# A shorter lead for the unit loads of a fused attention and feed-forward kernel, from the preparation of unit 11 on

## The chip, the cores and the metric

One core of one Trainium2 chip. The metric is the device time of one execution in microseconds (us). Most executions of one kernel agree within 0.3%, so each kernel was timed in several rounds, next to the kernel before on the same chip. A **ratio** in this document is the mean time of one kernel's fast runs over that of the other's of the same rounds, so it is not quite the ratio of the medians that are quoted beside it. Runs that fell into a slower state of the chip are left out of ratios.

The engines: PE multiplies matrices, PEld is its weight load, ACT and DVE do element-wise work, POOL is a further element-wise engine, SP issues nearly all DMAs. "SPq" in the profile is SP's sequencer. A DMA *lands* when all its data has arrived; its window on SP ends earlier. The *lead* is how many units ahead of the prepared one the loads are issued.

## The reference

Decaying linear attention over blocks, then a bilinear feed-forward layer. Cut to what matters:

```python
# q, k, v: (4, 8, 768, 64); lam: (8,)
for b in range(nb):                       # blocks of the sequence
    intra = (q_b @ k_b.T * Dmask) @ v_b   # decay within the block
    inter = (q_b * lam_pow) @ kv_state    # everything earlier
    out_b = intra + inter
    kv_state = lam_block * kv_state + (k_b * rev_pow).T @ v_b
x = out.reshape(3072, 512)
result = ((x @ w_a) * (x @ w_b)) @ w_out  # 512 -> 1536 -> 512
```

## The kernel before

The sequence is cut into 24 units of 128 rows (4 batches of 6). The units are put together in groups; while PE runs the feed-forward layer of one group, the attention of later units is slipped in at fixed slots of the plan. Each unit needs three loads (q, k, v, 256 KB each), a scaling of k and q on POOL, a cast of v on DVE, and a transpose of the scaled pair. From unit 11 on that transpose is a DMA. The parts that the change touches:

```python
GROUPS = (4, 1, 2, 4, 4, 4, 4, 1)
LOOKAHEAD = 3
DMA_T_FROM = 11
...
# plan of group 3 (units 7 to 10): slot, piece, unit. P prepares, S and Q hold scores
# (1, "P", 13), (3, "S", 11), (3, "S", 12), (3, "P", 14),
# (7, "Q", (11, 12, 13, 14)), (10, "P", 15), (12, "P", 16), (16, "Q", (13, 14, 15, 16))
...
ld_pool = tile_pool(name="ld", bufs=4)          # four buffers each for q, k, v
...
    def load_x(w, u):
        ...
        nc.sync.dma_start(out=t, in_={"q": qr, "k": kr, "v": vr}[w][b, nb])   # L126
...
    def pump():                                  # issues what may be issued now
        while pending:
            kind, c = pending[0]
            if kind in "abo":
                ...                              # weights, all done early on
            elif c >= used["u"] + LOOKAHEAD:
                return
            pending.pop(0)
            ...
                load_x(kind, c)
...
    def prep_k(u):
        make_ks(u, ...)                          # POOL, L257
        make_qs(u, "pool")                       # POOL, L262
        used["u"] = u + 1
        if u >= DMA_T_FROM:
            ...
            nc.sync.dma_start_transpose(...)     # L280

    def prep_v(u):
        make_vb(u, ...)                          # L271
        pump()                                   # loads of u + 3 follow the transpose of u
```

So SP meets, for each prepared unit u, first the transpose of u, then the three loads of unit u + 3, all in one in-order stream with the stores of the results.

## Time and profile before

| | |
|---|---|
| time of the first three runs | 235.88, 236.29, 240.94 us |
| median with later rounds of the same session | 236.31 us (6 runs) |
| span of the profiled execution | 234.4 us |
| PE busy | 226.4 us, 97% |
| wait of PE for a transposed unit | one, near 101 us |

The lines that carry this stand in the prediction below. The list of waits of PEld between 70 and 200 us of the kernel before has this line (total, times, longest):

```profile
PEld L308 <- DMA qkT<-qk: 1.5, 1, 1.5
```

The next two lines are busy time by stretch, one for 95 to 105 us and one for 86 to 98 us, of the kernel before. Columns: stretch, its length, then busy time and instructions of PE, PEld, DVE, ACT and POOL; the last two numbers are the share of 16 DMA engines and GB/s:

```profile
95.00:105.00 10.00, 8.68 (x74) 4.46 (x72) 6.57 (x11) 3.34 (x7) 2.04 (x2) 1.00 1.34 184
...
86.00:98.00 12.00, 12.00 (x70) 5.55 (x69) 7.96 (x13) 3.67 (x7) 4.09 (x4) 1.00 1.24 247
```

PE lacks 1.3 us in the first stretch. From 86 to 98 us the DMA engines are booked beyond their number (1.24) and move 247 GB/s. The share is the time that packets took, counted where they start; a high share alone doesn't prove a high rate.

### The profile page before, as it was taken

The numbers are of one execution on the slowest core, as the hardware profiler recorded it, in microseconds if no ns is written. First come the engines' busy times: TensorE is split into PE (matmuls) and PEld (weight loads), VectorE is DVE, ScalarE is ACT, GpSimd is POOL, SyncE is SP. The second block draws the span as 40 slices with busy tenths as digits, with TensorE's granted clock in tenths as the row PEclk, the third lists the DMA queues.
The fourth block names the chain that finished last, engine by engine and source line by source line (L and its number), as shares of the span: only waits on it lengthen the run. The fifth ranks groups of instructions, "written<-read, shape, count | busy, mean of one in ns | idle before, by whom it ended". The sixth has DMA issues, their size and how long they took to land.

```text
span 234.4 us, 4575 instructions
## 1 busy us (share of the span) xinstructions
PE 226.4 (97%) x1791; PEld 125.6 (54%) x1791; DVE 114.5 (49%) x204; ACT 93.0 (40%) x174; POOL 49.6 (21%) x65
## 2 busy tenths in 40 slices
PE   7799999999999999979999999999999999999994
PEld 2474444459689554444544454544454544444493
DVE  0896557536459627664144574135574224332050
ACT  3585753066364443332243342243342233432261
POOL 6061000237245544130333330030300000000000
PEclk9999999999999999999999999999999999999999
DMA  4999999999998999999719969415050220000311
GB/s 153 302 286 350 347 366 282 294 214 292 215 235 183 228 200 254 188 203 231 174 45 222 181 105 229 121 68 111 0 48 0 89 88 6 0 0 6 131 48 46
DMA packets 94278, 38.32 MB, mean 163 GB/s; under 512 B 81200, under 2 KB 89776, under 8 KB 94256
## 3 DMA queue, kind: packets, MB, share of 16 engines
q1 hardware_dynamic: 94112, 38.02, 70.8%
q8 instruction: 14, 0.23, 0.5%
q14 instruction: 8, 0.07, 0.1%
q10 hardware_dynamic: 144, 0.00, 0.0%
HBM read 28.32 MB, written 6.29 MB: 148 GB/s over the span
## 4 chain that ended last, share of the span: by engine, by line
PE 88%; DMA 6%; ACT 2%; DVE 1%; SPq 1%; issue 1%; DVEq 0%
PE op L453 26%; PE a_ps L432 26%; PE b_ps L432 25%; DMA k<-in_k_dram 3%; PE o_ps L350 3%; DMA qkT<-qk 2%; PE kq L308 2%; PE o_ps L340 2%; PE kvd L364 2%; PE tps L294 1%; DVE m L325 1%; ACT o_sb L448 1%; SPq L207 1%; PE kq L565 1%; ACT xT L357 0%
## 5 line engine op out<-in xcount | busy, mean ns | idle before, releaser
L444 DVE TENSOR_TENSOR ab<-a_sb,b_ps 128x512 bf16<-128x512 bf16 (+2 forms) x96 | 52.5, 552 | 80.9 <-PE b_ps L432 58.5
L432 PE MATMUL a_ps<-xT,wa_sb 128*128 128x512 bf16 (+2 forms) x384 | 77.2, 326 | 0.6 <-ACT xT L357 0.6
L432 PE MATMUL b_ps<-xT,wb_sb 128*128 128x512 bf16 (+2 forms) x384 | 77.3, 326 | 0.0
L439 ACT CAST a_sb<-a_ps 128x512 bf16<-128x512 f32 (+2 forms) x96 | 45.6, 481 | 62.4 <-PE a_ps L432 61.5
L453 PE MATMUL op<-wo_sb,ab 128*128 128x512 bf16 (+2 forms) x312 | 65.6, 363 | 0.0
L432 PEld LDWEIGHTS <-wb_sb 128*128 128x128 bf16 x384 | 34.5, 98 | 28.6
L432 PEld LDWEIGHTS <-wa_sb 128*128 128x128 bf16 x384 | 33.8, 98 | 29.0 <-POOL wa_sb L160 0.6
L453 PEld LDWEIGHTS <-ab 128*128 128x128 bf16 x312 | 28.7, 98 | 29.9
L325 DVE TENSOR_TENSOR m<-kq,lotri 128x512 bf16<-128x512 f32 x47 | 29.4, 682 | 19.0 <-PE kq L308 18.7
L257 POOL TENSOR_TENSOR qk<-kf,lp_k 128x512 bf16<-128x512 f32 x18 | 18.9, 1051 | 79.3 <-PE kvd L364 30.9
L448 ACT COPY o_sb<-op 128x512 f32<-128x512 f32 (+2 forms) x26 | 14.2, 554 | 37.8 <-PE op L453 37.8
L262 POOL TENSOR_TENSOR qk<-qf,lp_q 128x512 bf16<-128x512 f32 x20 | 21.0, 1051 | 23.0 <-DMA qf<-in_q_dram 23.0
L357 ACT CAST xT<-o_ps 128x512 bf16<-128x512 f32 x22 | 12.0, 590 | 18.4 <-PE o_ps L350 17.9
L396 DVE TENSOR_TENSOR st<-kvd,bdiag 128x512 bf16<-128x512 f32 x18 | 12.3, 682 | 4.9 <-PE kvd L364 3.8
L296 ACT COPY qkT<-tps 128x1024 bf16<-128x1024 bf16 x7 | 7.1, 1012 | 10.7 <-PE tps L294 10.7
L195 PE MATMUL idle<-idle_sb 128*128 128x128 bf16 (+1 forms) x31 | 7.4, 380 | 1.3 <-DVE idle_sb L190 1.3
L308 PE MATMUL kq<-qkT 64*128 64x128 bf16 x160 | 6.7, 218 | 1.3 <-DMA qkT<-qk 1.3
L350 PE MATMUL o_ps<-m,vb 128*64 128x128 bf16 x192 | 7.9, 222 | 0.0
L271 POOL CAST vb<-vf 128x512 bf16<-128x512 f32 x7 | 4.6, 651 | 14.1 <-DMA vf<-in_v_dram 12.8
L271 DVE CAST vb<-vf 128x512 bf16<-128x512 f32 x17 | 7.5, 441 | 0.0
L340 PEld LDWEIGHTS <-st 128*128 128x128 bf16 x80 | 5.4, 98 | 2.8
L350 PEld LDWEIGHTS <-vb 128*64 128x64 bf16 x192 | 5.8, 109 | 1.4
(56 smaller groups left out, 85.8 us busy)
## 6 DMA issues: line engine op xcount, KB each, us to landing
vf<-in_v_dram SPq DMA_DIRECT2D x24, 256.0 KB, 4.9
out_dram<-o_sb SPq DMA_DIRECT2D x23, 256.0 KB, 2.0
qf<-in_q_dram SPq DMA_DIRECT2D x20, 256.0 KB, 4.2
kf<-in_k_dram SPq DMA_DIRECT2D x20, 256.0 KB, 4.7
wst<-in_moe_w_a_dram SPq DMA_DIRECT2D x6, 512.0 KB, 8.8
wst<-in_moe_w_b_dram SPq DMA_DIRECT2D x6, 512.0 KB, 8.8
wst<-in_moe_w_out_dram SPq DMA_DIRECT2D x6, 512.0 KB, 8.5
q<-in_q_dram SPq DMA_DIRECT2D x2, 512.0 KB, 5.5
```

What stands on the lines that cost most here:

```text
L257: eng_of(eng).tensor_mul(qk[:, 1], raw.pop((u, "k")), lp_k[:, u % NB].to_broadcast([128, H, D]))
L262: eng_of(eng).tensor_mul(U[u]["qk"][:, 0], raw.pop((u, "q")), lp_q[:, u % NB].to_broadcast([128, H, D]))
L271: eng_of(eng).tensor_copy(vb, vf)
L325: nc.vector.tensor_mul(m, kq[i], lotri_bc)
L350: nc.tensor.matmul(d["o"][p, hp, :], lhsT=d["vb"][:, 2 * hp + i, :], rhs=d["m"](i, hp), start=(first and hp == 0), stop=True, skip_group_c ...
L357: nc.scalar.copy(xT[:, :, col:col + BLK], o_ps)
L396: nc.vector.tensor_mul(st[:].rearrange("p hp i d -> p hp (i d)"), ps[:].rearrange("p hp i d -> p hp (i d)"), bdiag_bc)
L432: nc.tensor.matmul(ps[:, :gt], lhsT=w_sb[:, s, f * 128:(f + 1) * 128], rhs=xT[:, s, :gt], start=(s == 0), stop=(s == KS - 1))
L439: nc.scalar.copy(a_sb[:, :gt], ps[:, :gt])
L444: nc.vector.tensor_mul(ab[:, f, :gt], a_sb[:, :gt], ps[:, :gt])
L448: nc.scalar.copy(o_sb[:, lo:hi], op[:, lo:hi])
L453: nc.tensor.matmul(op[:, lo:hi], lhsT=ab[:, f, t * 128:(t + 1) * 128], rhs=wo_sb[:, f, lo:hi], start=(f == 0), stop=(f == FC - 1))
```

## The change

The intent is to issue the loads of the later units closer to their use: from the preparation of unit 11 on, a unit's loads are issued when the unit two before it has been prepared, not three. Everything else stays.

```diff
-LOOKAHEAD = 3
+LOOKAHEAD = (3, 2)
...
-            elif c >= used["u"] + LOOKAHEAD:
+            elif c >= used["u"] + LOOKAHEAD[used["u"] > DMA_T_FROM]:
```

## The prediction

> **What bounds the kernel now.** I read the page first, then who waits for whom, then the timeline around the one wait that matters, then the sequencer that issues the DMAs. The page's first part says that the matrix engine is the bound:
>
> ```profile
> PE 226.4 (97%) x1791; PEld 125.6 (54%) x1791; DVE 114.5 (49%) x204; ACT 93.0 (40%) x174; POOL 49.6 (21%) x65
> ```
>
> The span is 234.4 us, so PE idles 8.0 us in all. Busy time by stretch puts 3.0 of these after 200 us (34.00 less 31.03) and the rest before 60 us, apart from one place: between 60 and 200 us only the stretches 95 to 100 (4.70 of 5.00) and 100 to 105 (3.98 of 5.00) are not full. The list of waits of PE, limited to 70 to 200 us, holds a single line:
>
> ```profile
> PE kq L308 <- DMA qkT<-qk: 1.3, 1, 1.3
> ```
>
> So everything that an earlier or later load of units 12 to 23 can give in the body of the kernel is this 1.3 us, unless it makes a new wait. The timeline shows it in the middle of the score products of two units, eight for unit 13 and eight for unit 14:
>
> ```profile
> 99.30 0.40 PE L308 MATMUL kq<-qkT 64*128 64x128 bf16 x8
> 101.02 0.40 PE L308 MATMUL kq<-qkT 64*128 64x128 bf16 x8 [1.32 <-DMA qkT<-qk]
> ```
>
> The data needed is the transposed q and k of unit 14 (the plan of group 3 has the scores of 13 and 14 at slot 7). The chain that ended last goes back to where that transpose came from:
>
> ```profile
> 95.14 5.84 DMA qkT<-qk
> 100.97 0.05 issue
> 101.02 0.40 PE kq L308 x8
> ```
>
> So the transpose of unit 14 started at 95.14 and took 5.84 us to land. Columns in the next fence: start in us, time, engine and line. The timeline of SP alone shows why it started so late. Each line is one DMA, L126 a load of q, k or v, L280 a transpose, L449 a store. Counting transposes from the first (unit 11), these are 11, 12, 13 and 14, and the triples of loads are units 14, 15 and 16:
>
> ```profile
> 79.38 2.94 SPq L280 DMA_TRANSPOSE qkT<-qk  x1
> 82.38 0.56 SPq L126 DMA_DIRECT2D qf<-in_q_dram  x1
> 82.99 0.58 SPq L126 DMA_DIRECT2D kf<-in_k_dram  x1
> 83.67 1.02 SPq L126 DMA_DIRECT2D vf<-in_v_dram  x1
> 84.79 0.85 SPq L449 DMA_DIRECT2D out_dram<-o_sb  x1
> 85.74 1.35 SPq L280 DMA_TRANSPOSE qkT<-qk  x1
> 87.14 0.57 SPq L126 DMA_DIRECT2D qf<-in_q_dram  x1
> 87.77 0.89 SPq L126 DMA_DIRECT2D kf<-in_k_dram  x1
> 88.75 0.73 SPq L126 DMA_DIRECT2D vf<-in_v_dram  x1
> 89.58 1.14 SPq L449 DMA_DIRECT2D out_dram<-o_sb  x1
> 90.83 1.67 SPq L280 DMA_TRANSPOSE qkT<-qk  x1
> 92.55 0.60 SPq L126 DMA_DIRECT2D qf<-in_q_dram  x1
> 93.20 0.70 SPq L126 DMA_DIRECT2D kf<-in_k_dram  x1
> 94.01 1.02 SPq L126 DMA_DIRECT2D vf<-in_v_dram  x1
> 95.14 2.32 SPq L280 DMA_TRANSPOSE qkT<-qk  x1
> ```
>
> The gaps between lines are 0.05 to 0.1 us: from 79.38 on SP issues without rest, in program order, and each instruction occupies it for 0.6 to 3 us. Yet the transpose's input was there long before, as the timeline of POOL shows for unit 14:
>
> ```profile
> 87.28 1.04 POOL L257 TENSOR_TENSOR qk<-kf,lp_k 128x512 bf16<-128x512 f32 x1 [3.18 <-PE a_ps L432]
> 88.28 1.04 POOL L262 TENSOR_TENSOR qk<-qf,lp_q 128x512 bf16<-128x512 f32 x1
> ```
>
> It was ready at 89.32 and waited 5.8 us for its turn. In this stretch **SP's issue order is the local bound**, not the data.
>
> **What the Trainium skill says.** "Perfetto Trace Analysis", section "DMA Instruction — HWDGE (DVE, Sync)": the profiled window of such a DMA begins when its semaphores are satisfied and ends when the sequencer is free again; the movement of the data lies outside. The trace agrees: the transpose has 2.32 us on SP and lands 5.84 us after its start. The same page, "What "DMA-bound" means", names a sequencer track that is solid DMA slices as one of the ways to be bound by DMA; the lines above are that. "DMA: Bandwidth & Descriptors", "Issuing engines are not separate DMA queues", calls the issue time usually small beside the DMA itself; here a triple of loads holds SP for 2.4 to 2.6 us against a landing of 3.5 to 6.1 us, so it is not small.
>
> **The change part by part.** No compute instruction is added or removed; the order of ACT and POOL is identical, and the differences on PE and DVE are buffer numbers. All 60 q, k and v loads of the later units remain. On SP each load triple from unit 14 on is issued one preparation step later: the order transpose 11, load 14, store, transpose 12, load 15, store, transpose 13, load 16, transpose 14 becomes transpose 11, store, transpose 12, load 14, store, transpose 13, load 15, transpose 14. So **one triple less stands ahead of transposes 12, 13 and 14**: about 2.45 us each (84.79 less 82.38 is 2.41, 89.58 less 87.14 is 2.44, 95.14 less 92.55 is 2.59). What was moved falls later into slack.
>
> The new times, with the durations shown: store at 82.4 (its copy on ACT ended at 81.24), transpose 12 at 83.3 (its input ended at 80.52), load 14 at 84.7 to 87.1, store at 87.1, transpose 13 at 88.3 (input ended at 84.10), load 15 at 90.0 to 92.5, transpose 14 not before 92.5. Its input now comes later too: k of unit 14 issues at about 85.3 and lands after 4.1 to 4.7 us (the landing times of k loads in this stretch), so 90.0; POOL then needs 1.04 for k and 1.0 for q, done at 92.1. Both conditions give 92.5 where it was 95.14, some 2.6 us earlier. With the same 5.84 us it lands at 98.4. PE reaches unit 14's products at 99.70 (101.02 less 1.32). The 1.32 us wait goes, with 1.3 us to spare.
>
> Is there a new wait? I followed each later unit. Unit 15: loaded by 97, POOL done at 97.4, needed at 116.3. Unit 16: load after transpose 14, data at 100, and POOL starts k at 102.45 anyway because it waits for PE to free a buffer. Units 17 and 18: loads at 100 and about 108, POOL took them up at 112.17 and 117.75. Unit 19: the load at 124.0 lands at 128.6, POOL ends at 131, its transpose ran at 135.93 because it waited 5.0 us for PE. Unit 20: issued at 128.7, lands at 133.5, POOL ends at 136, transpose at 139.76. Units 21 and 22: 142 and 147 against a transpose at 157.46 and a POOL start at 152.62. Unit 23: load after transpose 21, 158.8 to 161.2, lands at 166; its transpose waits for PE until about 170 anyway. It pushes transpose 22 from 158.84 to about 161.2, landing at 166, needed at 170.79. All have 3 us or more. **Sum: 1.3 us off, 0 on**, so 236.3 becomes 235.0.
>
> **The rivals.** First, **the load becomes the wait**: with only two units of lead, unit 14's k load may land late, POOL is late and transpose 14 issues at 95 or after. For it: POOL waited for a k load four times in the whole run (6.6 us), one of them just before (1.49 us at 82.01), and the wait ahead of k of unit 14 ended at 87.28, just when the load of 82.99 with its 4.1 us landed. Against: there are 2.6 us of gain to eat up first. It would give 236 to 238. Second, **the DMA engines and not SP are the bound**: the DMA share of the stretches from 80 to 110 is above 1.2, and SP's windows of 2 to 3 us for a transpose look like back-pressure. Then transpose 12, directly behind transpose 11 and a store, would take up to 2.9 instead of 1.35 us, transpose 14 would start at about 94 and land at 99.7, and the gain would be near zero to 1.3: 235.0 to 236.2. In its favour for the change, less data stands ahead of transpose 14 in that case too, since 768 KB of loads are moved behind it. Third, a lucky case: beyond the wait, fewer collisions speed up nothing on PE, as its products run at a fixed pitch (0.86 us for four) and its clock is full; so no gain over 1.5 us is plausible.
>
> **Range and chances.** Median before is 236.29, of three runs of which one (240.94) stands apart; the two others average 236.1. I take 235.0. Low end 234.3: full gain from the lower of the two fast runs would be 234.6, less 0.3 for scatter. High end 236.4: no gain, or a partial gain and scatter. Within 2% means 231.6 to 241.0: a gain over 4.7 us has no idle time to come from, so faster gets 0.01; a loss over 4.7 us needs several new stalls or a slow run as median: 0.02.
>
> **What would show it.** Right: PE has no wait at line 308 between 70 and 200 us, busy time is full from 95 to 105, transpose 14 starts near 92.5 and lands before 99, and everything after 100 us is earlier by 1.3 us to the end, with a span near 233.1. Wrong: a wait for the transpose remains (then look whether POOL or SP held it), or a new wait of PE for a transpose appears near 116, 134, 151 or 170, or POOL waits for loads on the way to a late transpose.

## The result, and the profile after

| | before | after |
|---|---|---|
| median | 236.31 us (6 runs, 235.88 to 240.94) | 234.57 us (6 runs, 234.51 to 234.68) |
| span in the profile | 234.4 us | 232.9 us |
| ratio of fast runs, 95% interval | | 0.9927, 0.9913 to 0.9941 |

The gain is 0.7%: real, as the interval shows, and within the 2% that count as the same.

The list of waits of PE between 70 and 200 us no longer has a line for a transpose. The timeline of PE in the kernel after shows the scores of units 13 and 14 as one run of 16 products where there were two of eight:

```profile
99.02 0.39 PE L340 MATMUL o_ps<-qkT,st 128*128 128x128 bf16 x4
99.34 0.62 PE L308 MATMUL kq<-qkT 64*128 64x128 bf16 x16
99.89 0.64 PE L350 MATMUL o_ps<-m,vb 128*64 128x128 bf16 x16
```

In the kernel before, the first eight products began at 99.30 and those of L350 at 101.34; here they begin at 99.34 and 99.89. So 1.49 us vanish in this one place (2.04 from products to L350 before, 0.55 after). That is the whole difference of the spans, 1.5 us. Busy time by stretch, kernel after, the same two stretches:

```profile
95.00:105.00 10.00, 9.95 (x79) 5.12 (x79) 7.50 (x12) 3.90 (x7) 3.70 (x4) 1.00 1.36 207
...
86.00:98.00 12.00, 11.95 (x70) 5.51 (x69) 8.07 (x13) 3.71 (x7) 4.46 (x4) 1.00 1.27 246
```

PE is full (9.95 of 10.00). From 86 to 98 us the DMA engines are as full as before: the work has changed its order, not its amount. The two microseconds after that stretch differ; they are taken up after the experiment act_beside. The timeline of SP in the kernel after shows the new order (L280 transposes 11, 12, 13, 14; L126 the loads of units 14 and 15; L449 stores):

```profile
79.05 2.12 SPq L280 DMA_TRANSPOSE qkT<-qk  x1
81.30 0.48 SPq L449 DMA_DIRECT2D out_dram<-o_sb  x1
81.89 2.08 SPq L280 DMA_TRANSPOSE qkT<-qk  x1
84.02 0.57 SPq L126 DMA_DIRECT2D qf<-in_q_dram  x1
84.64 0.63 SPq L126 DMA_DIRECT2D kf<-in_k_dram  x1
85.37 0.90 SPq L126 DMA_DIRECT2D vf<-in_v_dram  x1
86.37 0.88 SPq L449 DMA_DIRECT2D out_dram<-o_sb  x1
87.35 1.33 SPq L280 DMA_TRANSPOSE qkT<-qk  x1
88.73 0.57 SPq L126 DMA_DIRECT2D qf<-in_q_dram  x1
89.35 1.01 SPq L126 DMA_DIRECT2D kf<-in_k_dram  x1
90.45 0.84 SPq L126 DMA_DIRECT2D vf<-in_v_dram  x1
91.41 2.12 SPq L280 DMA_TRANSPOSE qkT<-qk  x1
```

Transpose 14 starts at 91.41, 3.7 us earlier than before, and takes 4.5 us to land in place of 5.84. It lands at 95.9, and PE needs it at 99.6 (99.34 and half of the 0.55 us that the 16 products take). What the shorter lead costs is visible on POOL, which now waits longer for k loads, among them those of unit 14 (first line) and of unit 19 (third):

```profile
88.96 1.23 POOL L257 TENSOR_TENSOR qk<-kf,lp_k 128x512 bf16<-128x512 f32 x1 [5.09 <-DMA kf<-in_k_dram]
90.16 1.04 POOL L262 TENSOR_TENSOR qk<-qf,lp_q 128x512 bf16<-128x512 f32 x1
...
127.79 1.29 POOL L257 TENSOR_TENSOR qk<-kf,lp_k 128x512 bf16<-128x512 f32 x1 [9.46 <-DMA kf<-in_k_dram]
```

POOL is done with unit 14 at 91.20, 0.2 us before SP turns to its transpose, and with unit 19 at 130.08, while its transpose starts at 134.47. Nothing on PE waits for either.

### The profile page after: what moved, and what is told of

Read it like the earlier page. It is cut to its first block, busy times and chain, and to the rows that moved or that the text cites. A ratio compares the mean times of both kernels' runs of the same rounds, so it can differ in the third digit from the quotient of the medians.

```text
span 232.9 us, 4552 instructions
## 1 busy us (share of the span) xinstructions
PE 224.7 (96%) x1768; PEld 125.6 (54%) x1791; DVE 116.0 (50%) x204; ACT 92.9 (40%) x174; POOL 50.3 (22%) x65
## 4 chain that ended last, share of the span: by engine, by line
PE 92%; DMA 3%; ACT 2%; issue 1%; SPq 1%; DVE 0%
PE a_ps L432 27%; PE b_ps L432 27%; PE op L453 26%; DMA k<-in_k_dram 3%; PE o_ps L350 3%; PE kq L308 2%; PE o_ps L340 2%; PE kvd L364 2%; PE tps L294 1%; ACT o_sb L448 1%; SPq L207 1%; PE kq L565 1%; ACT xT L357 0%; PE kv L364 0%; PE tk L529 0%
## 5 line engine op out<-in xcount | busy, mean ns | idle before, releaser
L453 PE MATMUL op<-wo_sb,ab 128*128 128x512 bf16 (+2 forms) x300 | 64.1, 362 | 0.9 <-issue 0.5
L262 POOL TENSOR_TENSOR qk<-qf,lp_q 128x512 bf16<-128x512 f32 x20 | 21.5, 1076 | 23.4 <-DMA qf<-in_q_dram 23.4
L271 DVE CAST vb<-vf 128x512 bf16<-128x512 f32 x17 | 9.3, 549 | 0.0
L350 PE MATMUL o_ps<-m,vb 128*64 128x128 bf16 x192 | 7.9, 222 | 0.0
L340 PEld LDWEIGHTS <-st 128*128 128x128 bf16 x80 | 5.4, 98 | 2.8
L350 PEld LDWEIGHTS <-vb 128*64 128x64 bf16 x192 | 5.8, 109 | 1.4
```

Of the source, the lines that this page charges most:

```text
L262: eng_of(eng).tensor_mul(U[u]["qk"][:, 0], raw.pop((u, "q")), lp_q[:, u % NB].to_broadcast([128, H, D]))
L271: eng_of(eng).tensor_copy(vb, vf)
L350: nc.tensor.matmul(d["o"][p, hp, :], lhsT=d["vb"][:, 2 * hp + i, :], rhs=d["m"](i, hp), start=(first and hp == 0), stop=True, skip_group_c ...
L453: nc.tensor.matmul(op[:, lo:hi], lhsT=ab[:, f, t * 128:(t + 1) * 128], rhs=wo_sb[:, f, lo:hi], start=(f == 0), stop=(f == FC - 1))
```

## The experiments

The theories. **A**: SP works through its DMAs in order, and the time that it spends on issuing loads 14 to 16 is what delays transpose 14. **C**: the later loads (units 17 to 23) share in the gain. **D**: what helped is that loads 14 and 15 no longer crowd transposes 12 and 13. **E**: the DMA engines are the limit, and data of loads ahead of or beside the transpose delays it, whoever issues them.

Twelve runs on the chip, all with correct results. "T14" is transpose 14: its start on SP, its time to land, and the wait of PEld for a transpose in the profile.

| run | T14 start | to land | wait | median | before, same rounds | ratio |
|---|---|---|---|---|---|---|
| before (first profile) | 95.14 | 5.8 | 1.5 | 236.31 | | |
| after | 91.41 | 4.5 | none | 234.57 | 236.31 | 0.9927 |
| before_again | 95.38 | 6.1 | 2.0 | 236.33 | 236.23 | 0.9967 |
| head_only | 91.30 | 4.6 | none | 234.61 | 236.23 | 0.9904 |
| tail_only | 95.28 | 5.7 | 1.4 | 236.20 | 236.23 | 0.9963 |
| one_triple | 92.4 | 4.1 | none | 234.68 | 236.23 | 0.9909 |
| load14_late | 95.75 | 5.6 | 1.8 | 236.04 | 235.68 | 1.0021 |
| act_queue | 94.6 | 6.7 | 1.5 | 235.85 | 235.68 | 1.0007 |
| two_all | 94.11 | 6.4 | none | 235.16 | 235.68 | 0.9977 |
| one_ahead | 94.58 | 4.7 | 0.8 (T16) | 235.59 | 235.68 | 0.9998 |
| act_beside | 92.4 | 7.1 | none | 234.22 | 235.91 | 0.9934 |
| small_issues | 94.11 | 5.5 | none | 235.05 | 235.90 | 0.9966 |
| small_again | 93.97 | 6.3 | 0.8 | 235.03 | 235.91 | 0.9970 |
| pool_queue | after 98 | | 5.7 | 241.17 | 235.90 | 1.0196 |

The rounds of the first four (236.23) had three runs of before at 238.2 to 238.8 us that pull the ratios down: the unchanged kernel itself came out at 0.9967 there. For these four the medians are the better guide. The kernel before has a median of 235.68 to 236.31 us, depending on the rounds, so a run is best compared with its own rounds.

### before_again: the same kernel once more

No edit but a comment.

> The unchanged kernel, profiled once more. Theory A (issue order on SP delays transpose 14): transpose 14 starts at about 95 us again and PE waits for it around 101 us; the length of that wait varies from run to run, by up to 1 us either way of 1.5 us, which would explain why the timed gain (1.7 us) is larger than the wait in the one profile (1.5 us) and why the kernel before scatters more than the changed one. Rival: the wait is an accident of the one profile; then it is absent here and the gain comes from elsewhere. Time 236.3 us under both.

The wait is there again, and longer (waits of PEld between 70 and 200 us):

```profile
PEld L308 <- DMA qkT<-qk: 2.0, 1, 2.0
```

The span is 234.9 us where the first profile had 234.4: the 0.5 us of extra wait is the 0.5 us of extra span. So the wait is no accident, its length varies with the execution, and between these two executions that variation goes straight into the time. The kernel after has no such wait; its six runs lie within 0.17 us.

### head_only and tail_only: which part of the change does it

```diff
 head_only
-            elif c >= used["u"] + LOOKAHEAD:
+            elif c >= used["u"] + (2 if 12 <= used["u"] <= 14 else LOOKAHEAD):
 tail_only
-            elif c >= used["u"] + LOOKAHEAD:
+            elif c >= used["u"] + (2 if used["u"] >= 15 else LOOKAHEAD):
```

> Two units of lead at the preparations of units 11, 12 and 13 only, and again three from unit 15 on: the order on SP is that of the changed kernel up to transpose 14, and that of the kernel before from transpose 15 on. Theory A: the whole gain, 234.6 us, ratio 0.993, transpose 14 starts near 91.5 us and PE has no wait for it. Rival C (the later loads, units 17 to 23, share in the gain because the DMA engines are less loaded there): only a part, 235.0 to 236 us.

> The complement: three units of lead up to the preparation of unit 13, two from unit 14 on. The order on SP up to transpose 14 is that of the kernel before. Theory A: no gain, 236.3 us, ratio 1.000 within 0.002, transpose 14 near 95 us, the PE wait of about 1.5 us stays. Rival C: a part of the gain, 235 to 236 us.

The head alone gives 234.61 us, the tail alone 236.20 us, where the change as a whole gave 234.57 and the kernel before 236.23 in these rounds. The timeline of PE of the tail-only kernel still has the gap:

```profile
99.38 0.40 PE L308 MATMUL kq<-qkT 64*128 64x128 bf16 x8
101.02 0.40 PE L308 MATMUL kq<-qkT 64*128 64x128 bf16 x8 [1.24 <-DMA qkT<-qk]
```

C falls. Of all the loads that the change moves, only those of units 14, 15 and 16 count.

### one_triple and load14_late: which loads, and where they stand

```diff
 one_triple: loads 16 go from ahead of transpose 14 to behind it
+            elif c >= used["u"] + (2 if used["u"] == 14 else LOOKAHEAD):
 load14_late: loads 14 go from ahead of transpose 12 to behind it
+            elif c >= used["u"] + (2 if used["u"] == 12 else LOOKAHEAD):
```

> Three units of lead throughout, except that the loads of unit 16 move from ahead of transpose 14 to behind it. Only one triple of loads changes its place. Theory A: SP reaches transpose 14 one triple earlier, about 92.5 us against 95.1, it lands by 98.4 and the wait is gone: 234.6 to 234.9 us. Rival D (what helped is that loads 14 and 15 no longer crowd transposes 12 and 13): the wait stays and the time is near 236.3 us.

> Only the loads of unit 14 move one step later (behind transpose 12 instead of ahead of it); loads 14, 15 and 16 all still stand ahead of transpose 14. Theory A: transpose 14 starts at 94 to 95 us as in the kernel before, the PE wait stays for the most part (0.7 to 1.5 us), 235.5 to 236.3 us. Rival D (relief of transposes 12 and 13 is what counts): the gain is there, 234.6 us.

Moving the three loads of unit 16 by one place gives 234.68 us: the gain in full but for 0.1 us. Moving those of unit 14, so that transpose 12 is relieved but all three triples still stand ahead of transpose 14, gives nothing, and if anything 0.2% the other way. D falls. What matters in these runs is whether three triples or two are issued between transposes 11 and 14; two_all below fits this too.

### act_queue: SP relieved, the data still ahead

```diff
-        nc.sync.dma_start(out=t, ...)
+        (nc.scalar if u == 16 else nc.sync).dma_start(out=t, ...)
```

> Three units of lead as before, but the three loads of unit 16 are issued by ACT instead of SP, at the same place in the program. The same data is on its way ahead of transpose 14; only SP is relieved of issuing it. Theory A (SP's issue order): transpose 14 starts near 92.5 us, right behind transpose 13, and lands before 99.4: no PE wait, 234.6 to 235.0 us. Rival E (the DMA engines' backlog: the data of the loads ahead delays the transpose, whoever issues it): transpose 14 starts earlier but still lands near 100.9 us, a landing of 8 us in place of 5.8, and 236 us remain. The three issues occupy ACT for 2 to 3 us, which PE should not feel.

This went against my theory A. SP has nothing between transposes 13 and 14 any more, and the time is that of the kernel before (1.0007). The timeline of this kernel, SP first, then ACT:

```profile
89.00 2.54 SPq L449 DMA_DIRECT2D out_dram<-o_sb  x1
91.64 5.61 SPq L280 DMA_TRANSPOSE qkT<-qk  x2
```

```profile
87.48 0.41 ACTq L126 DMA_DIRECT2D qf<-in_q_dram  x1
88.06 0.46 ACTq L126 DMA_DIRECT2D kf<-in_k_dram  x1
88.64 2.29 ACTq L126 DMA_DIRECT2D vf<-in_v_dram  x1
```

ACT issues load 16 earlier than SP did, from 87.5 on. In exchange SP's own windows grow: the store to 2.54 us (1.14 before), the two transposes to 5.61 us together (3.11 in one_triple, where load 16 is not ahead). Transpose 14 starts at 94.6 and needs 6.7 us to land. The expectation of E, a start that is earlier and a landing that is longer, fits better than A's, though E had not foreseen that SP's windows would be stretched as well. So SP's solid track is here not shown to be a limit of its own. But load 16 is also issued some 5 us earlier than in the kernel before; the next run comes closer in this.

### act_beside: SP relieved, the data beside

Load 16 is issued by ACT as above, but at the preparation of unit 14 (the edit of one_triple is added). Against one_triple only the issuing engine of load 16 changes, and with it the time of its issue.

> Load 16 issued by ACT again, but at the preparation of unit 14, so that ACT issues it at about 91.5 to 93.5 us, beside transpose 14 (SP, about 92.4) and not ahead of transpose 13. SP has nothing between transposes 13 and 14. If SP's issue time alone were the cause (A): transpose 14 starts at 92.4 and lands by 97, no wait, 234.7 us. If data under way at the same time is as bad as data ahead (E): its window is stretched beyond 2 us and it lands near 100, some wait remains, 235 to 236 us.

```profile
90.73 3.52 SPq L280 DMA_TRANSPOSE qkT<-qk  x2
```

Transpose 14 starts at 92.4 as in one_triple. It lands after 7.1 us in place of 4.1: the 3.0 us are the effect of load 16 moving at the same time, and SP has no issue of load 16 to make. It lands at 99.5, just when PE wants it (its 16 products begin at 99.26), so the time is as good as with the change (0.9934 against 0.9927). The longer landing is what E foresaw, but no wait remained; in the time it was A's figure (234.7) that came closer.

A check of the size: load 16 has 3 x 256 KB = 786 thousand bytes. This kernel moves 223 GB/s from 86 to 98 us, so load 16 occupies the DMA engines for an estimated 3.5 us, worked out from these two numbers (3.2 us at the 246 GB/s of the kernel after). The 3.0 us are of that size.

The kept traces show something more, which no run here was made to test. Busy time from 98 to 100 us in the kernel before, with transpose 14 under way and PE waiting at the end, then from 94 to 96 us in the kernel after, where its transpose 14 is in its last microseconds:

```profile
98.00:100.00 2.00, 1.70 (x18) 0.83 (x15) 0.96 (x3) 0.59 (x1) 0.00 (x0) 1.00 1.44 72
...
94.00:96.00 2.00, 2.00 (x12) 0.88 (x10) 2.00 (x4) 0.58 (x1) 1.56 (x2) 1.00 1.23 243
```

In the kernel before, the share is high (1.44), yet little moves. Packets that start from 98.0 to 98.5 us take so long that they book the engines five times over (5.02), and from 98.5 to 99.5 us only 11 GB/s start. In all five profiles of before, before_again, tail_only, load14_late and act_queue, where PE waits for transpose 14, there is such a microsecond, of 5 to 22 GB/s, before it lands. In the five of after, head_only, one_triple, two_all and act_beside, where PE doesn't wait for it, the slowest microsecond between its start and its landing has 65 GB/s or more. (The runs with small DMAs, pool_queue and one_ahead are left aside.) The kernel after has a slow microsecond later, 45 GB/s from 99.5 to 100.5 us, when transpose 14 has long landed. So "the engines are full" doesn't describe the last part of the late landing: there the engines stall for about as long as PE waits. The stall is not the whole delay either, since two_all, without it, lands at 100.5. What brings it about, and whether it is cause or companion of the delay, stays open.

### small_issues and small_again: SP occupied, little data

```diff
 on top of one_triple, in prep_k(14), ahead of the transpose
+        for i in range(4):
+            nc.sync.dma_start(out=<small tile 128x8>, in_=lam, each row the same 32 bytes)
```

> The order of the kernel with load 16 moved behind transpose 14, and in the place that the three loads left, four small DMAs of 4 KB on SP: the sequencer is occupied again for some 2 us, but 16 KB move in place of 768 KB. Theory A (the time that SP spends on issuing): transpose 14 starts at 94 to 95 us and lands as late as in the kernel before, near 101; the wait is back, 235.5 to 236 us. Theory E (the data ahead on the shared DMA engines): transpose 14 may start later than 92.4, but it lands in 4.1 to 4.6 us, by 99.4, and there is no wait: 234.6 us. In between, start and landing are two terms that add.

> The kernel with four small issues in the place of load 16, once more, because its runs lay between 234.5 and 236.9 us. Transpose 14 starts near 94.1 us; if its landing is 5.5 us again it comes within 0.5 us of the time that PE needs it (99.4 to 99.7) and the runs scatter between 234.5 and 235.5; if it is 4.1 to 4.6 us the wait is absent in every run and the time is 234.6.

The result lies between, 235.05 and 235.03 us, and the runs scatter (234.5 to 236.9, and one at 238.3). The four issues hold SP for 2.0 to 2.3 us, so transpose 14 starts 1.6 to 1.7 us later than in one_triple. But it also lands late, and the reason spoils the experiment. The DMA view of small_again from 94 to 98 us, in 40 slices:

```profile
DMA  0000000000000000000000000000000000000000
...
DMA packets 421, 0.01 MB, mean 3 GB/s; under 512 B 421, under 2 KB 421, under 8 KB 421
```

The substitute was not cheap. For 4 us the DMA engines are nearly idle while 421 tiny packets trickle through, at 3 GB/s, and transpose 14 lands only after them. So these two runs show that SP's own time delays the start, as A has it: by 1.6 to 1.7 us for issues that hold SP for 2.0 to 2.3 us. They don't show what the landing would have been without data ahead. How much of the 2.7 us of later start in the kernel before (95.14 against 92.4) is SP's own time and how much is stretched by the engines stays open: SP's windows for a transpose are 1.24 us on a quiet queue (one_ahead) and 1.35 to 2.98 us in the busy stretch.

### pool_queue: the data by a third queue

The same edit as act_queue with `nc.gpsimd`.

> The reverse: three units of lead, and the loads of unit 16 issued by POOL, so neither SP nor the hardware queues issue them, while their 768 KB still move ahead of transpose 14 (POOL reaches them at about 84 us). Theory A: SP comes to transpose 14 right behind 13, near 92.5, it lands by 99.4, no wait, 234.6 us. Theory E: transposes 13 and 14 take longer to be issued and to land, as when ACT issued the loads; the wait stays, 235.5 to 236.3 us.

It is 2% slower by its fast runs (ratio 1.0196, 95% interval 1.0152 to 1.0240), which counts as unclear at the 2% threshold. Only one of its six runs has the full clock; the others have 0.986 to 0.993. That one is its best, 238.57 us, and still worse than anything that either theory had put down. Its profile (clock 0.986): SP's v load of unit 15 took 5.61 us to issue, and transposes 13 and 14 started after 98 us.

```profile
91.38 5.61 SPq L126 DMA_DIRECT2D vf<-in_v_dram  x1
97.09 1.08 SPq L449 DMA_DIRECT2D out_dram<-o_sb  x1
98.28 2.89 SPq L280 DMA_TRANSPOSE qkT<-qk  x2
```

This is against A once more: SP had fewer issues to make and was held up longer. Why POOL's queue is this much worse than ACT's isn't settled here.

### one_ahead and two_all: how short the lead may be

```diff
 one_ahead
+            elif c >= used["u"] + (1 if used["u"] > DMA_T_FROM else LOOKAHEAD):
 two_all
+            elif c >= used["u"] + 2:
```

> One unit of lead from unit 12 on. This is the other rival of the prediction, that a shorter lead makes the loads themselves the wait. By the arithmetic of the prediction the landing of a k load (4.5 us), POOL (2.1 us) and the transpose (4.5 us) now stand one behind the other between two transposes of SP: transpose 14 lands near 99.5, just in time, but transpose 16 lands near 118 where PE needs it at 115.3, and transposes 20 and 22 are late by some 5 us each. Expected 240 to 248 us; if the lead of one is enough, 234.6.

> Two units of lead for all units, the early ones too. Theory A says nothing of gain here: PE has no wait for loads before 70 us, so at best 234.6 us. POOL already waits for k loads between 62 and 82 us with a lead of three; with two these waits grow, and if the 1 to 2 us of slack of units 9 and 10 are used up, PE waits there: 234.6 to 238 us. It tells why the change keeps three units for the early ones.

My expectation for a lead of one was a clear miss: 235.59 us, level with the kernel before, in place of 240 to 248. There is one wait, for transpose 16. The timeline of PE of this kernel:

```profile
114.81 0.40 PE L308 MATMUL kq<-qkT 64*128 64x128 bf16 x8
115.88 0.40 PE L308 MATMUL kq<-qkT 64*128 64x128 bf16 x8 [0.67 <-DMA qkT<-qk]
```

It costs 0.8 us, and the profile's span of 233.7 us is 0.8 longer than that of the kernel after. I had counted the landing of the transpose, 4.5 us, into the round of one unit (4.5 + 2.1 + 4.5 = 11.1 us). It doesn't belong there: SP goes on to the next loads when its own window of the transpose, 1.24 to 1.30 us, is over. After the transpose of 122.05 the k load is issued at 124.02 and takes 4.2 us, POOL ends at 130.63, and the next transpose starts at 130.66. The round takes 8.1 to 8.6 us per unit (transposes at 122.05, 130.66, 138.80, 147.26). PE uses up four units in 34.8 us (in the kernel before, the chain has the first feed-forward products of group 4 at 121.60 and those of group 5 at 156.37), or 8.7 us for one. So even a lead of one keeps pace, once the first shortage is over.

With two for all units (two_all) the wait for transpose 14 is gone too, but PE arrives 0.9 us late at its place: the products of L340 that stand at 99.02 in the kernel after begin at 99.90. POOL's waits for k loads between 50 and 100 us add up to 20.5 us. The list of waits of PE of this kernel shows a third of the 0.9 us directly:

```profile
PE o_ps L340 <- DVE st L396: 0.3, 1, 0.3
```

The absence of the wait is thus no merit of the shorter lead. Transpose 14 starts at 94.11 and lands at 100.5, just when the late PE comes to it (100.22 and half of 0.55); at the place of the kernel after, 99.6, PE would have waited some 0.9 us. Here too three triples (13, 14 and 15) are issued between transposes 11 and 14.

235.16 us is between the two kernels, as expected. Keeping three for the early units is right.

## Why the prediction was right, point by point

- **The result.** 234.57 us stands against 235.0, inside 234.3 to 236.4, and "same" had 0.97. The time says little on the mechanism: it would be the same for any landing of transpose 14 up to 99.6 us, so the errors in its start and its landing (below) could not show in it. That part was luck.
- **Where the gain could come from.** "Everything that an earlier or later load of units 12 to 23 can give in the body of the kernel is this 1.3 us": right in place. The gain is this one wait, as head_only and tail_only show. The term was mis-sized: PE's idle time in the record is 1.32 us, but the loss is 1.49 us by the starts of the instructions around it, which is what PEld's line says (1.5). In other executions it is more (2.0 in before_again), so the 1.7 us of the timed medians are no contradiction.
- **The order on SP.** "One triple less stands ahead of transposes 12, 13 and 14": right, and one_triple and load14_late show that for transpose 14 two triples in place of three make the gain. The start came at 91.41 where 92.5 was worked out; load 14 was issued at 84.02 rather than 84.7, since transpose 11 took 2.12 us and not 2.94, and POOL was done at 91.20 rather than 92.1.
- **The landing.** "With the same 5.84 us it lands at 98.4": too long. It took 4.5 us and landed at 95.9. The margin is 3.7 us, not 1.3. One triple behind the transpose instead of ahead shortens its landing as well as its queue.
- **"SP's issue order is the local bound, not the data."** The order was the right lever, the reason given was only half right, and this is the step that failed. With SP relieved and the data kept ahead (act_queue), nothing was gained; with the data kept beside (act_beside), the landing grew by 3.0 us. SP's own time does count for the start (1.6 to 1.7 us in the two runs with small DMAs). The second rival, which named the DMA engines, was the better description of the landing; its number (a transpose 14 at 94, a gain of near zero to 1.3 us) was too pessimistic. It was right in part on transpose 12, which took 2.08 us on SP, between the 1.35 us of the prediction and the rival's 2.9. Neither text foresaw the stall before the landing (11 GB/s from 98.5 to 99.5 us in the kernel before); it stays unexplained.
- **The first rival, the load as the wait.** It did not come true. POOL waits 5.09 us for k of unit 14, as feared, but ends 0.2 us before SP gets to the transpose. Even a lead of one costs only 0.8 us of span against the kernel after.
- **The slack of the later units.** Confirmed in the main: POOL was done with units 19 and 20 at 130.1 and 134.3 (131 and 136 worked out), transpose 22 followed load 23 at 159.69 (161.2 worked out), and PE has no wait for any of them. "All have 3 us or more" was not what the prediction's own figures gave: unit 16, with data at 100 and POOL at 102.45, had 2.45 us.

## What to carry to other kernels

When a DMA on the path of the bounding engine is late, look at what stands ahead of it in its queue and whether that is needed as soon: here an early prefetch was not free where DMA traffic was dense, and moving one unit's loads behind the urgent transfer gained nearly all there was to gain. A sequencer track that is solid with DMA slices does not prove that the sequencer is the limit; test it by issuing part of the work elsewhere. Here that gained nothing while the data still went ahead of the transfer (act_queue). Look also at what is moved in the last microseconds before the landing: a window that ends too early (86 to 98 us here) misses a stall. And shorten a lead only in the stretch where its slack was worked out: here the same shortening for the early units gave back 0.6 us of the span (233.5 against 232.9).

## What the Trainium skill lacked or had wrong

- "Perfetto Trace Analysis", section "DMA Optimizations", says that balancing DMAs over the engines that can issue them may help if the issuing engine looks busy with slices as opposed to actual DMA time. Solid slices do not tell the two apart. SP was solid here, yet issuing three of its loads from ACT gave a ratio of 1.0007 and from POOL 1.0196 (unclear); SP's windows just grew (a store from 1.14 to 2.54 us). The page "DMA: Bandwidth & Descriptors", section "Issuing engines are not separate DMA queues", is the one that the runs bear out.
- "Advanced Engine Details and Errata", section "X-Bar Transpose (TRN2)", calls transpose DMAs as fast as regular ones. On a quiet queue (one_ahead, 122 to 126 us) that holds: 3.2 us to land for a transpose, 3.6 to 4.4 us for loads of 256 KB. No page says how far a transpose stretches next to loads: 4.1 to 7.3 us here.
- "Perfetto Trace Analysis", section "Summary: the profiler window per engine type", says that the end of a PE instruction is an estimate. What that means for reading a gap: the idle time recorded on PE was 1.32 us where the starts of the instructions show 1.49 us lost. How much of the 0.17 us is the estimate and how much the overlap of matmuls is not shown.
- No page that I read tells what DMAs of a few bytes per row do to a transfer behind them: four DMAs of 4 KB in rows of 32 bytes left the DMA engines at 3 GB/s for 4 us.
- No page that I read tells, for DMAs within one core, of a stall of the DMA engines around a transpose, as in the kernel before from 98.5 to 99.5 us (11 GB/s).
